# A ring of three banks, an argmax in six pieces partly on GpSimd, and another order in the attention's steps

## The chip, the cores and the metric

One core of one Trainium2 chip runs the kernel. The metric is the device time of one execution in microseconds, as the median of several runs. Below, PE is TensorE (PEld its weight loads), DVE is VectorE, ACT is ScalarE, POOL is GpSimd and SP is SyncE, whose queue issues nearly all DMAs.

## What is computed

A clustered attention, followed by two mixer layers that the change doesn't touch. The attention, for two batches of 8 heads, 768 positions and 64 numbers a head:

```
q_assign = np.argmax(np.einsum('bhsd,hcd->bhsc', q_n, c_n), axis=-1)
k_assign = np.argmax(np.einsum('bhsd,hcd->bhsc', k_n, c_n), axis=-1)
mask = q_assign[:, :, :, None] == k_assign[:, :, None, :]
scores = scale * np.matmul(q, k.transpose(0, 1, 3, 2))
scores = np.where(mask, scores, -1000000000.0)
scores = scores - np.max(scores, axis=-1, keepdims=True)
attn = np.exp(scores)
attn = attn / (np.sum(attn, axis=-1, keepdims=True) + 1e-09)
return np.matmul(attn, v).astype(np.float32)
```

Here `q_n`, `k_n` and `c_n` are the normed queries, keys and 16 centroids of a head. A position sees only the positions whose nearest centroid is the same as its own. The mixers are products of the result with `moe_*` and then `moe2_*` weights.

## The kernel before

Products of float32 numbers are made from a high part (rounded to fp32r) and a low part (what the rounding left over), so each tile is first split in two: ACT rounds, and DVE or POOL subtracts.

The attention runs over 8 pairs of heads (G = 8), and a pair is 12 steps of one tile of 128 query rows (NTT = 12, NTILE = 96 steps). The order of each engine's work is the order in which the program writes it; nothing is scheduled behind it. In `step(n)` the program writes: the score product of tile n+2 (`s_mm`) into one of two pairs of PSUM banks, its row maximum on DVE (`s_max`), the exponential of tile n+1 on ACT (`s_exp`) into one of three `p32` buffers, the six 128x128 transposes of tile n on PE (`t_mm`), four to a bank in two banks (TB), the split of each full bank (`t_out`: ACT writes `pth`, then DVE writes `ptl`), then the actions in `mid`, then two of the six chunks of the product with v of the three tiles before (`pv`, into bank OB, copied by `pv_out` after the third step), then the actions in `late`. Since six blocks fill one and a half banks, even and odd steps differ: an even step completes one bank, an odd step two.

`mid` and `late` are lists by step, filled by `at`: `merge` (12 small products that turn the result into rows, bank MB) and `merge_out` at two steps of each pair, `zmm` and `zadd` for the first mixer's low-rank part, and the preparation of a later pair. With s1 the first step of the pair ahead of pair n, that preparation is: load q and k (`load_pair`, s1-6), the products with the centroids (`scores`, s1-2), the high parts of q and k on ACT (s1-2 and s1-1), the transposition of the products to `am1` (`scores_out`) and the argmax on DVE (`argmax_a` at s1-1, `argmax_b` at s1), the low part of k on POOL (s1) and of q on DVE (s1+1), the mask rows (`mask_rows`, POOL, s1+1), and the DMAs that stack the parts into `qS` and `kS` (`stack`: eight for the high, six for the low parts, eight for the mask, on SP). The value tile is loaded at s1+3 and split at s1+5 (`v_split`: both halves on ACT, then on POOL).

The argmax takes the largest of each 16 products, marks the places that reach it, weighs the marks so that the first one wins, takes the largest again, marks it, and transposes the marks. Lines of the profile: 73 is every matrix product, 276 the transposes, 262 the row maximum, 267 the exponential, 78 every rounding on ACT, 85 every subtraction, 193 to 207 the argmax, 175 the load of v, 170 that of q.

## Time and profile before

| what | us |
|---|---|
| median of 3 runs (lowest, highest) | 872.11 (870.2, 873.57) |
| the profiled execution | 874.27 |
| its span, first to last instruction | 872.3 |
| PE busy in the span | 793.5 (91%) |
| DVE busy | 542.7 (62%) |
| ACT busy | 353.4 (41%) |
| POOL busy | 102.1 (12%) |

The mean granted clock of PE is 0.973 over the span. Shares over the span mix stages: the attention's steps run from 22 to 330 us, the mixers after that. Matmuls are pipelined, so a busy PE is not PE at its peak; how much of a stretch is lost is read from the waits ahead of its instructions and from the granted clock.

### The profile page before, as it was taken

Reading aid. Unit: us, or ns where it says so; the run is one execution under the profiler, and the core shown is the slowest. Engines: PE = TensorE matmul, PEld = TensorE weight load, DVE = VectorE, ACT = ScalarE, POOL = GpSimd, SP = SyncE. Lnnn points to the kernel's source line nnn. Section 1 sums busy time; section 2 is a strip of 40 time slices with the busy share of each in tenths; the row PEclk is TensorE's granted clock in tenths of the full one; section 3 lists DMA queues with packets and bytes.
Section 4 is the critical chain, followed back from the end, with each engine's and each line's share of the span. In section 5 each row is a group of like instructions: output and inputs, shape, how many; then the busy total and the mean of one; then the engine's idle time right before and its main releaser. Section 6 shows DMA issues by size and latency. Waiting matters only on the chain.

```text
span 872.3 us, 11264 instructions
## 1 busy us (share of the span) xinstructions
PE 793.5 (91%) x3989; PEld 666.1 (76%) x3989; DVE 542.7 (62%) x873; ACT 353.4 (41%) x687; POOL 102.1 (12%) x96
## 2 busy tenths in 40 slices
PE   1798888989889989988879999999999999999998
PEld 0677787878778877766558888788888888888886
DVE  3788868687787887888898687684233124113113
ACT  1686766667576664434333333342212121111110
POOL 1210101011110011000012232221210021000000
PEclk9998999999999989999989999999999999999999
DMA  8645334252535024888888999996444433754752
GB/s 209 138 109 136 73 100 92 81 116 79 151 80 153 25 97 146 279 284 285 286 291 309 367 354 393 390 388 231 145 153 166 140 125 132 276 194 159 274 193 96
DMA packets 59239, 167.79 MB, mean 192 GB/s; under 512 B 8656, under 2 KB 16848, under 8 KB 59184
## 3 DMA queue, kind: packets, MB, share of 16 engines
q1 hardware_dynamic: 57984, 164.95, 58.2%
q10 hardware_dynamic: 1200, 2.13, 1.0%
q8 instruction: 31, 0.51, 0.2%
q14 instruction: 24, 0.20, 0.1%
HBM read 114.10 MB, written 32.51 MB: 168 GB/s over the span
## 4 chain that ended last, share of the span: by engine, by line
PE 62%; DVE 23%; DMA 5%; ACT 4%; SPq 4%; issue 2%; DVEq 0%; ACTq 0%
PE ps L73 58%; PE ps L276 4%; DVE ptl L85 3%; DVE nm L262 3%; DVE c L104 3%; DVE c L105 3%; DVE qk L85 2%; ACT qk L78 2%; DVE c L100 2%; DVE c L103 2%; DMA qk<-scr_a 2%; DVE am L199 1%; DMA vraw<-in_v_dram 1%; SPq L239 1%; SPq L238 1%
## 5 line engine op out<-in xcount | busy, mean ns | idle before, releaser
L73 PE MATMUL ps<-gh,qk 128*128 128x512 f32 x672 | 223.7, 394 | 1.2 <-DMA qk<-scr_a 1.2
L610 DVE SCALAR_TENSOR_TENSOR gl<-ps,gh 128x512 fp32r<-128x512 f32 x84 | 57.9, 689 | 192.9 <-ACT gh L609 192.9
L73 PEld LDWEIGHTS ps<-gh,qk 128*128 128x128 f32 x672 | 127.2, 189 | 27.8 <-ACT gh L609 1.6
L609 ACT ACTIVATE gh<-ps 128x512 fp32r<-128x512 f32 x84 | 49.9, 594 | 225.8 <-PE ps L73 222.7
L73 PE MATMUL ps<-gl,qk 128*128 128x512 f32 x336 | 133.3, 397 | 4.0 <-DVE gl L610 3.4
L276 PE MATMUL ps<-ident,p 128*128 128x128 f32 x576 | 90.6, 290 | 27.0 <-DVE ptl L85 26.7
L73 PE MATMUL ps<-qk 112*128 112x384 f32 (+1 forms) x384 | 93.0, 368 | 23.4 <-ACT p L267 11.4
L262 DVE TENSOR_REDUCE nm<-ps 128x1 f32<-128x768 f32 x96 | 91.3, 951 | 28.4 <-PE ps L73 28.0
L85 DVE TENSOR_TENSOR ptl<-ps,pth 128x512 fp32r<-128x512 f32 x144 | 94.9, 685 | 21.5 <-ACT pth L78 18.3
L276 PEld LDWEIGHTS ps<-ident,p 128*128 128x128 f32 x576 | 73.1, 149 | 39.1 <-DVE ptl L85 35.4
L267 ACT ACTIVATE p<-ps,nm 128x768 f32<-128x768 f32 x96 | 86.5, 902 | 31.3 <-DVE nm L262 30.5
L78 ACT ACTIVATE pth<-ps 128x512 fp32r<-128x512 f32 x144 | 81.6, 597 | 43.1 <-PE ps L276 42.7
L73 PEld LDWEIGHTS ps<-qk 112*128 112x128 f32 (+1 forms) x384 | 74.8, 208 | 31.2 <-ACT p L267 18.2
L73 PE MATMUL ps<-qk,qk 128*128 128x512 f32 x336 | 86.2, 400 | 10.2 <-ACT qk L78 10.2
L73 PEld LDWEIGHTS ps<-qk,qk 128*128 128x128 f32 x336 | 61.0, 188 | 31.0 <-ACT qk L78 14.6
L73 PEld LDWEIGHTS ps<-gl,qk 128*128 128x128 f32 x336 | 63.6, 189 | 21.2 <-DVE gl L610 8.8
L73 PE MATMUL ps<-pth,vhl 128*128 128x384 f32 x192 | 76.7, 400 | 0.6 <-ACT osb L292 0.6
L73 PE MATMUL ps<-u2h,qk 128*128 128x512 f32 x224 | 74.1, 392 | 0.0
L73 PE MATMUL ps<-u1h,qk 128*128 128x512 f32 x224 | 73.9, 391 | 0.0
L78 ACT ACTIVATE qk<-c 128x512 fp32r<-128x512 f32 x56 | 35.3, 631 | 93.5 <-DVE c L105 60.6
L73 PE MATMUL ps<-ptl,vhl 128*128 128x384 f32 x192 | 68.5, 357 | 1.3 <-DVE ptl L85 1.3
L85 POOL TENSOR_TENSOR qk<-c,qk 128x512 fp32r<-128x512 f32 x28 | 39.5, 1410 | 150.9 <-ACT qk L78 150.9
(133 smaller groups left out, 1031.8 us busy)
## 6 DMA issues: line engine op xcount, KB each, us to landing
qk<-scr_b SPq DMA_DIRECT2D x72, 512.0 KB, 3.3
qk<-scr_a SPq DMA_DIRECT2D x64, 512.0 KB, 7.7
c<-in_wa_dram SPq DMA_DIRECT2D x32, 512.0 KB, 5.4
scr_a<-qk SPq DMA_DIRECT2D x32, 512.0 KB, 5.2
c<-in_wb_dram SPq DMA_DIRECT2D x24, 512.0 KB, 7.2
scr_b<-qk SPq DMA_DIRECT2D x24, 512.0 KB, 6.9
qk<-sq__84 SPq DMA_DIRECT2D x15, 384.0 KB, 3.9
qk<-sk__85 SPq DMA_DIRECT2D x29, 192.0 KB, 3.0
```

What stands on the lines that cost most here:

```text
L73: pe.matmul(o, lhsT=l, rhs=r, start=start, stop=stop, **kw)
L78: act.activation(o, i, AF.Copy, scale=scale)
L85: eng.tensor_tensor(out=o, in0=a, in1=b, op=ALU.subtract)
L100: dve.tensor_scalar(out=dst, in0=dst, scalar1=2.0 ** -15, scalar2=122879.9921875, op0=ALU.max, op1=ALU.min)
L103: dve.tensor_scalar(out=d, in0=d, scalar1=3, scalar2=0x3FFFFFF8, op0=ALU.logical_shift_left, op1=ALU.bitwise_and)
L104: dve.scalar_tensor_tensor(out=d, in0=lo, scalar=29, in1=d, op0=ALU.logical_shift_right, op1=ALU.bitwise_or)
L105: dve.scalar_tensor_tensor(out=d, in0=hi, scalar=-0x40000000, in1=d, op0=ALU.bitwise_and, op1=ALU.bitwise_or)
L262: dve.tensor_reduce(out=nm[:, n % 4 : n % 4 + 1], in_=ps[:, b0 : b0 + 2, 0:HS], axis=AX.XY, op=ALU.max, negate=True)
L267: act.activation(p32[n % NP32].rearrange("p (j k) -> p j k", j=2), ps[:, b0 : b0 + 2, 0:HS], AF.Exp, bias=nm[:, n % 4 : n % 4 + 1], accum_ ...
L276: pe.transpose(ps[:, TB + j % 2, ts(i, P)], p32[n % NP32][:, ts(c, P)], ident)
L609: act.activation(gh, o, AF.Relu)
L610: dve.scalar_tensor_tensor(out=gl, in0=o, scalar=0.0, in1=f32(gh), op0=ALU.max, op1=ALU.subtract)
```

## The change

`NP32` is 4. Transposes, `merge`, `scores`, `zmm` and `zadd` take their bank from a ring of banks 4, 5 and 6 in the order in which the program writes them; `pv` accumulates in bank 7. `t_out` is divided into `t_hi` (ACT) and `t_lo` (DVE). The argmax becomes `arg0` to `arg4`, which with `mask_rows` lie in different steps; in pairs 1 to 7 `arg1` and `arg3` run on POOL, where a comparison is a subtraction and a test of its sign. The preparation of a pair begins earlier (`load_pair` at s1-8, `scores` at s1-5), the load of v moves from s1+3 to s1-1, and the split of v is done in two halves, at s1+5 and s1+7. Pair 1's argmax is spread over steps 0 to 5, and its mask is stacked at step 6. `step` has one order for even steps and another for odd ones: in an even step `mid` runs right behind the score product and `late` ahead of `t_lo`; in an odd step two transposes come first, and the first `t_hi` comes ahead of the exponential.

```diff
-    NP32 = 3
+    NP32 = 4
...
-    def v_split(g):
+    def v_split(g, a):
         o, i = vhl[g % 2], vraw.rearrange("p c (a d) -> p a c d", a=2)
-        for a in range(2):
-            rnd(act, o[:, a, :, 0:D], i[:, a])
-            sub(pool, o[:, a, :, D:], i[:, a], f32(o[:, a, :, 0:D]))
+        rnd(act, o[:, a, :, 0:D], i[:, a])
+        sub(pool, o[:, a, :, D:], i[:, a], f32(o[:, a, :, 0:D]))
 
     held = {}
 
...
         p = g % NPAIR
-        held["sc"] = bk
+        held["sc"] = bk = ring()
         for qd in range(4):
             src = (Rq, Rk)[qd // 2]
             mm(ps[32 * qd : 32 * qd + 32, bk, 0:HS], zc[:, ts(p, 32)], src[:, ts(qd % 2, HS)], True, True)
...
 
-    def argmax_a():
-        v1 = am1.rearrange("p (g c) -> p g c", c=16)
-        v2 = am2.rearrange("p (g c) -> p g c", c=16)
+    v1 = am1.rearrange("p (g c) -> p g c", c=16)
+    v2 = am2.rearrange("p (g c) -> p g c", c=16)
+    v3_ = am3.rearrange("p (g c) -> p g c", c=16)
+    best = lambda: amx.unsqueeze(2).to_broadcast([P, 24, 16])
+
+    def arg0():
         dve.tensor_reduce(out=amx, in_=v1, axis=AX.X, op=ALU.max)
-        dve.tensor_tensor(out=v2, in0=v1, in1=amx.unsqueeze(2).to_broadcast([P, 24, 16]), op=ALU.is_ge)
-        dve.tensor_tensor(out=v2, in0=v2, in1=wcl.unsqueeze(1).to_broadcast([P, 24, 16]), op=ALU.mult)
-
-    def argmax_b():
-        v2 = am2.rearrange("p (g c) -> p g c", c=16)
-        v3_ = am3.rearrange("p (g c) -> p g c", c=16)
+
+    def arg1(eng):
+        w = wcl.unsqueeze(1).to_broadcast([P, 24, 16])
+        if eng is pool:
+            sub(pool, v1, v1, best())
+            pool.tensor_scalar(out=am2, in0=am1, scalar1=0.0, scalar2=None, op0=ALU.is_ge)
+            pool.tensor_tensor(out=v2, in0=v2, in1=w, op=ALU.mult)
+        else:
+            dve.tensor_tensor(out=v2, in0=v1, in1=best(), op=ALU.is_ge)
+            dve.tensor_tensor(out=v2, in0=v2, in1=w, op=ALU.mult)
+
+    def arg2():
         dve.tensor_reduce(out=amx, in_=v2, axis=AX.X, op=ALU.max)
-        dve.tensor_tensor(out=v3_, in0=v2, in1=amx.unsqueeze(2).to_broadcast([P, 24, 16]), op=ALU.is_equal)
+
+    def arg3(eng):
+        if eng is pool:
+            sub(pool, v2, v2, best())
+            pool.tensor_scalar(out=am3, in0=am2, scalar1=0.0, scalar2=None, op0=ALU.is_ge)
+        else:
+            dve.tensor_tensor(out=v3_, in0=v2, in1=best(), op=ALU.is_equal)
+
+    def arg4():
         dve.transpose(out=ohT, in_=am3)
 
     def mask_rows(eng):
...
 
-    TB, OB, MB = 4, 6, 7
+    OB = 7
+    banks, tb = [4, 5, 6], {}
+
+    def ring():
+
+        banks.append(banks.pop(0))
+        return banks[-1]
 
     def t_mm(n, c0, c1):
         for c in range(c0, c1):
             j, i = divmod(NS * n + c, 4)
-            pe.transpose(ps[:, TB + j % 2, ts(i, P)], p32[n % NP32][:, ts(c, P)], ident)
-
-    def t_out(j):
-        o = ps[:, TB + j % 2, :]
+            if i == 0:
+                tb[j] = ring()
+            pe.transpose(ps[:, tb[j], ts(i, P)], p32[n % NP32][:, ts(c, P)], ident)
+
+    def t_hi(j):
+        rnd(act, pth[:, ts(j % (NBL // 2), 4 * P)], ps[:, tb[j], :])
+
+    def t_lo(j):
         r = ts(j % (NBL // 2), 4 * P)
-        rnd(act, pth[:, r], o)
-        sub(dve, ptl[:, r], o, f32(pth[:, r]))
+        sub(dve, ptl[:, r], ps[:, tb[j], :], f32(pth[:, r]))
 
     def pv(k, c):
         g, h, a, _ = tinfo(NT * k)
...
 
-    def merge(g, h):
+    def merge(g, h, bk=None):
+        held["mg"] = bk = bk or ring()
         for t in range(NT):
             for a in range(2):
-                mm(ps[:, MB, t * P + a * D : t * P + a * D + D], osb[a][:, ts(t, P)], ii, True, True)
+                mm(ps[:, bk, t * P + a * D : t * P + a * D + D], osb[a][:, ts(t, P)], ii, True, True)
 
...
                     stack(0, a, what, (sp, act)[a], *l)
-            scores(0, MB)
+            scores(0)
             load_pair(1, act)
             scores_out()
-            argmax_a()
-            argmax_b()
+            arg0()
+            arg1(dve)
+            arg2()
+            arg3(dve)
+            arg4()
             mask_rows(dve)
             for a in range(2):
...
                 stack(1, a, "hi", sp)
-            v_split(0)
+            for a in range(2):
+                v_split(0, a)
             load_v(1)
             s_mm(0)
             s_mm(1)
             s_max(0)
             s_max(1)
-            scores(1, OB)
+            scores(1)
             scores_out()
             q_lo(dve, Rq)
...
             at(late, s, lambda g=g, h=h: merge_out(g, h))
         if g + 1 < G:
-            at(mid, s0 + NTT + 5, lambda g=g: zmm(g, MB))
+            at(mid, s0 + NTT + 5, lambda g=g: zmm(g, ring()))
             at(late, s0 + NTT + 5, lambda g=g: zmm_out(g))
         n, s1 = g + 1, s0
         if 2 <= n < G:
-            at(late, s1 - 6, lambda g=n: load_pair(g))
-            at(mid, s1 - 2, lambda g=n: scores(g, MB))
-            at(late, s1 - 2, q_hi)
-            at(late, s1 - 1, k_hi)
-            at(late, s1 - 1, scores_out)
-            at(late, s1 - 1, argmax_a)
-            at(late, s1, argmax_b)
-            at(late, s1, lambda: k_lo(pool, Rk))
-            for a in range(2):
-                at(late, s1, lambda g=n, a=a: stack(g, a, "hi", sp))
+            at(late, s1 - 8, lambda g=n: load_pair(g))
+            at(mid, s1 - 5, lambda g=n: scores(g))
+            at(late, s1 - 5, scores_out)
+            at(late, s1 - 4, q_hi)
+            at(late, s1 - 4, arg0)
+            at(late, s1 - 3, lambda: arg1(pool))
+            at(late, s1 - 2, k_hi)
+            at(late, s1 - 2, arg2)
+            at(late, s1 - 1, lambda: arg3(pool))
+            at(late, s1 - 1, lambda: k_lo(pool, Rk))
+            at(late, s1, arg4)
+            at(late, s1, lambda: q_lo(dve, Rq))
             at(late, s1 + 1, lambda: mask_rows(pool))
-            at(late, s1 + 1, lambda: q_lo(dve, Rq))
-            for a in range(2):
-                at(late, s1 + 2, lambda g=n, a=a: stack(g, a, "lo", sp))
-                at(late, s1 + 2, lambda g=n, a=a: stack(g, a, "mask", sp))
+            for what, s in (("hi", -2), ("lo", 1), ("mask", 2)):
+                for a in range(2):
+                    at(late, s1 + s, lambda g=n, a=a, w=what: stack(g, a, w, sp))
         if n < G:
             if n > 1:
-                at(late, s1 + 3, lambda g=n: load_v(g))
-            at(late, s1 + 5, lambda g=n: v_split(g))
+                at(late, s1 - 1, lambda g=n: load_v(g))
+            for a in range(2):
+                at(late, s1 + 5 + 2 * a, lambda g=n, a=a: v_split(g, a))
 
     for t in range(NS):
         s = NTT * 4 + 7 + 6 * t
-        at(mid, s, lambda t=t: zadd(0, t, MB))
-        at(late, s, lambda t=t: zadd_out(0, t, MB))
-    at(late, 0, argmax_a)
-    at(late, 1, argmax_b)
-    at(late, 1, lambda: mask_rows(dve))
+
+        def za(t=t):
+            held["za"] = ring()
+            zadd(0, t, held["za"])
+
+        at(mid, s, za)
+        at(late, s, lambda t=t: zadd_out(0, t, held["za"]))
+    for s, f in ((0, arg0), (1, lambda: arg1(pool)), (2, arg2), (3, lambda: arg3(pool)), (4, arg4), (5, lambda: mask_rows(pool))):
+        at(late, s, f)
     for a in range(2):
-        at(late, 1, lambda a=a: stack(1, a, "mask", sp))
+        at(late, 6, lambda a=a: stack(1, a, "mask", sp))
     at(late, 2, load_uv)
...
 
     def step(n):
-        if n + 2 < NTILE:
-            s_mm(n + 2)
-            s_max(n + 2)
-        if n + 1 < NTILE:
-            s_exp(n + 1)
+        k, r = divmod(n, NT)
         j, i = divmod(NS * n, 4)
-        t_mm(n, 0, 4 - i)
-        t_out(j)
-        t_mm(n, 4 - i, NS)
-        if i:
-            t_out(j + 1)
-        for f in mid.get(n, ()):
-            f()
-        k, r = divmod(n, NT)
-        if k:
-            for c in range(2 * r, 2 * r + 2):
-                pv(k - 1, c)
-            if r == 2:
+
+        def run(d):
+            for f in d.get(n, ()):
+                f()
+
+        def heads():
+            if n + 2 < NTILE:
+                s_mm(n + 2)
+
+        def maxima():
+            if n + 2 < NTILE:
+                s_max(n + 2)
+
+        def exps():
+            if n + 1 < NTILE:
+                s_exp(n + 1)
+
+        def pvs(*cs):
+            if k:
+                for c in cs:
+                    pv(k - 1, 2 * r + c)
+
+        def pvo():
+            if k and r == NT - 1:
                 pv_out(k - 1)
-        for f in late.get(n, ()):
-            f()
+
+        if i == 0:
+            heads()
+            run(mid)
+            t_mm(n, 0, 4)
+            pvs(0, 1)
+            maxima()
+            t_mm(n, 4, NS)
+            exps()
+            t_hi(j)
+            pvo()
+            run(late)
+            t_lo(j)
+        else:
+            t_mm(n, 0, 2)
+            heads()
+            maxima()
+            t_mm(n, 2, NS)
+            t_hi(j)
+            pvs(0)
+            t_lo(j)
+            pvs(1)
+            run(mid)
+            exps()
+            t_hi(j + 1)
+            t_lo(j + 1)
+            pvo()
+            run(late)
 
 
...
     hidden(0)
-    merge(G - 1, 1)
+    merge(G - 1, 1, 6)
     merge_out(G - 1, 1)
```

## Rows read from the trace of the kernel before

**Rows 1.** Stretches: length, busy time and instructions by engine, clock, DMA share, GB/s.

```profile
22.00:330.00 308.00, 268.85 (x1670) 242.73 (x1669) 249.61 (x377) 209.53 (x427) 36.96 (x32) 0.93 0.40 101
...
212.55:250.21 37.66, 33.45 (x216) 30.00 (x215) 30.79 (x48) 25.35 (x53) 4.46 (x4) 0.95 0.41 101
```

**Rows 2.** Timeline, TensorE's weight loads: start us, us, engine, line, what, count.

```profile
153.50 0.72 PEld L73 LDWEIGHTS ps<-qk 112*128 112x128 f32 x4
154.21 0.76 PEld L276 LDWEIGHTS ps<-ident,p 128*128 128x128 f32 x6
...
155.57 0.73 PEld L73 LDWEIGHTS ps<-qk 112*128 112x128 f32 x4
...
170.70 1.42 PEld L73 LDWEIGHTS ps<-ii,osb 128*128 128x128 f32 x12
```

**Rows 3.** PE's waits (us, times, longest): 22-330; 60-285 (two rows); 285-330.

```profile
PE ps L276 <- DVE ptl L85: 26.7, 17, 4.6
...
PE ps L276 <- DVE ptl L85: 17.6, 11, 4.6
PE ps L73 <- ACT p L267: 9.4, 6, 2.0
...
PE ps L276 <- DVE ptl L85: 5.2, 3, 2.4
```

**Rows 4.** Timeline of one argmax burst; in brackets: idle before, and what ended it.

```profile
179.47 1.83 POOL L85 TENSOR_TENSOR sk__85<-sk__85 128x768 fp32r<-128x768 f32 x1 [15.16 <-ACT sk__85 L78]
...
180.07 1.65 DVE L199 TENSOR_TENSOR am<-am,amx 128x384 bf16<-128x384 f32 x1
...
181.75 0.36 DVE L200 TENSOR_TENSOR am<-am,wcl 128x384 bf16<-128x384 bf16 x1
...
182.03 0.95 DVE L262 TENSOR_REDUCE nm<-ps 128x1 f32<-128x768 f32 x1
...
182.90 0.68 DVE L85 TENSOR_TENSOR ptl<-ps,pth 128x512 fp32r<-128x512 f32 x1
...
183.63 0.66 PE L276 MATMUL ps<-ident,p 128*128 128x128 f32 x4 [2.10 <-DVE ptl L85]
...
184.07 0.56 DVE L206 TENSOR_TENSOR am<-am,amx 128x384 bf16<-128x384 bf16 x1
```

**Rows 5.** Timeline around one load and split of v.

```profile
158.20 0.58 SPq L175 DMA_DIRECT2D vraw<-in_v_dram  x1
...
161.75 0.94 ACT L78 ACTIVATE vhl<-vraw 128x384 fp32r<-128x384 f32 x2 [1.23 <-DMA vraw<-in_v_dram]
...
163.62 1.51 PE L73 MATMUL ps<-qk 112*128 112x384 f32 x4 [1.96 <-ACT p L267]
```

**Rows 6.** Stretches at clock 0.50: two of ten, and all ten's sum.

```profile
163.81:167.22 3.41, 3.41 (x14) 3.32 (x14) 2.49 (x4) 2.50 (x6) 0.50 (x1) 0.50 0.00 0
...
320.82:327.65 6.83, 6.83 (x32) 6.73 (x31) 3.25 (x8) 2.90 (x7) 0.00 (x0) 0.50 0.09 34
sum 40.96, PE 39.30 PEld 37.53 DVE 32.06 ACT 24.04 POOL 3.83; mean PE 3.93 PEld 3.75 DVE 3.21 ACT 2.40 POOL 0.38
```

**Rows 7.** Groups by line, 212.55 to 250.21: count, busy us, mean ns, idle before.

```profile
L267 ACT ACTIVATE p<-ps,nm 128x768 f32<-128x768 f32 x12 | 10.8, 902 | 3.8 <-DVE nm L262 3.8
L78 ACT ACTIVATE pth<-ps 128x512 fp32r<-128x512 f32 x18 | 10.2, 596 | 5.2 <-PE ps L276 5.1
...
L85 POOL TENSOR_TENSOR vhl<-vraw,vhl 128x384 fp32r<-128x384 f32 x2 | 2.0, 1004 | 15.0 <-ACT vhl L78 15.0
...
L210 POOL TENSOR_SCALAR om<-ohT,msk 128x384 f32<-128x384 bf16 x1 | 0.7, 665 | 4.1 <-DVE ohT L207 4.1
```

**Rows 8.** Two lines on DVE: duration ns min/median/max, first and last start.

```profile
L199 DVE TENSOR_TENSOR am<-am,amx x8: 557/1646/1647, 10.9 to 254.9; 128x384 bf16<-128x384 f32 x8
...
L85 DVE TENSOR_TENSOR ptl<-ps,pth x142: 674/681/693, 30.0 to 326.1; 128x512 fp32r<-128x512 f32 x142
```

**Rows 9.** DMA issues, 22 to 330: KB each, median us to landing.

```profile
sq__84<-in_qT_dram SPq DMA_DIRECT2D x6, 384.0 KB, 3.9
```

## Prediction before the change was run

> **What bounds the kernel now.** The whole change lies in the attention stage, so I first read the busy time by stretch, then who waited for whom on TensorE inside that stage, then the clock granted there, and last one period of the timeline, to see which instruction stood late in which queue.
>
> The attention steps run from about 22 to 330 us, 308 of the 872. In that stretch TensorE is busy 269 us and the clock is 0.93 on average [rows 1]. In one pair's period of 37.66 us TensorE is busy 33.45, VectorE 30.79, ScalarE 25.35, GpSimd 4.46. No engine is full, but three are loaded, and each takes its work in program order. A step that nothing disturbs takes 155.57 - 153.50 = 2.07 us from one score product to the next, 0.71 of it the product and about 0.76 the six transposes [rows 2]; twelve of them are 24.8 us, and two merges of 1.42 raise it to 27.7. The rest of the period is small products and loss.
>
> Where the loss is: TensorE waited 26.7 us in 17 waits for `ptl`, the low half that VectorE takes out of a transpose bank [rows 3]. From 60 to 285 us these are 17.6 us in 11 waits, and beside them 9.4 us in 6 waits for ScalarE's exponential; from 285 to 330 us 5.2 us in 3. The two kinds have different causes.
>
> One: the argmax burst. `argmax_a` stands on VectorE as a block behind `scores_out` and ahead of the next row maximum. Its comparison takes 1.65 us while GpSimd runs `k_lo` (1.83), so the row maximum starts only at 182.03, the low half behind it at 182.90, and TensorE, whose only two transpose banks are both still to be read, sits idle 2.10 us until 183.63 [rows 4]. Six such waits stand between 60 and 285 us, the longest 4.6: 4.6 + 5 x 2.1 = 15.1 of the 17.6 us. The other five waits are short, 2.5 us together. Before 60 us 26.7 - 17.6 - 5.2 = 3.9 us of the same kind are left, from pair 1's argmax.
>
> Two: the v split. SyncE issues the load of v at 158.20, last behind the whole stack of the pair; ScalarE waits 1.23 us for it at 161.75, the exponential queues behind the split, and TensorE idles 1.96 us [rows 5]. Six times, 9.4 us.
>
> Three: the clock. Ten stretches, 40.96 us together, have a granted clock of 0.50 (1.2 GHz of 2.4); the one at 163.81 begins just after the wait that ended at 163.62 [rows 6]. Half of 40.96, some 20.5 us, is lost to that.
>
> **The change part by part.** *Ring of three banks.* Transposes get a third bank, the small products (merge, z, scores) share the ring, and `pv` keeps a bank of its own (7). With two banks a transpose needs the low half of two uses before; now of three. In even steps `late` stands ahead of `t_lo` on VectorE, which is a delay there, but only bank reuse three allocations later, or `pv` in the odd steps that begin a group, waits for that. I count the argmax waits as gone by this and the next part together and leave the five short ones (2.5 us) in.
>
> *Argmax.* VectorE loses three of its operations in each of pairs 2 to 7 and in pair 1: 1.65 + 0.36 + 0.56 = 2.57 us a pair [rows 4], 1.09 of it the time in which the comparison was held (it takes 0.557 at its shortest [rows 8]). Its load falls to 28.2 us a pair. GpSimd gets five: a subtraction of 384 columns (1.00 for the same size in `vhl`), a comparison (0.67 as `mask_rows`), a product (1.00), then a subtraction and a comparison: 2.67 and 1.67 us, 4.34 a pair [rows 7]. With its 4.46 it is busy some 9 of 33 us, so they lie beside other work. A comparison on GpSimd isn't in the trace: from below it is 0.67, from above 1.83, the longest GpSimd operation near it, though that has twice the columns [rows 4]; I take 0.67, the row of the same form. "GPSIMD Engine Reference", section 3.1, of the Trainium skill says that branching on data costs about 12 cycles an element; an estimate from it is 3.8 us for one comparison of 384 at its 1.2 GHz, which no run here shows, and with it the two GpSimd blocks would take 5.8 and 4.8 us instead of 2.7 and 1.7.
>
> The new waits: `arg2` and `arg4` on VectorE wait for GpSimd, and behind them in VectorE's queue stand the low half of an even step, and behind that the next row maximum, for which ScalarE and then TensorE wait. `arg2` is two steps behind `arg0`, one of them with a merge: 2 x 2.07 + 1.42 = 5.6 us for 2.67 us of work. `arg4` is two steps behind `arg2`: 4.1 us for 1.67. Both have more than 2 us to spare, so I cost them at nothing; without that cover each microsecond is a microsecond of the pair.
>
> *v split.* The load of v moves ahead of the low and mask stacks on SyncE's queue, past 14 issues of about 0.58 each [rows 5], so it lands some 8 us earlier against a wait of 1.23. The split becomes two pieces of half the length two steps apart. The six waits, 9.4 us, go. What is late next is the exponential behind one half of the split, in an odd step, where TensorE has transposes and a small product left.
>
> *SyncE's order.* `load_pair` goes from step -6 to -8 and `scores` from -2 to -5. Counted from `k_hi` at -2, the queue holds 7 + 1 + 6 + 8 issues and then the two loads, 24 x 0.58 = 13.9 us, plus 3.9 to land [rows 9]: 17.8 us. The scores come nine steps later, with one merge between: 9 x 2.07 + 1.42 = 20.0 us. It is covered by some 2 us and by the z product of that stretch; beyond that each late microsecond would stand on TensorE, with everything that is queued behind the scores. Pair 1's masks move from step 1 to 6; their eight issues take 8 x 0.58 = 4.6 us and are wanted at step 10, four steps or 8.3 us later. I cost it at nothing; without that cover it is a single wait.
>
> *Order in the step.* In an odd step ScalarE now has the high half of a two-block bank ahead of the exponential. Its chain is: two of the six transposes 0.25, high half 0.60, exponential 0.90 [rows 2, 7], 1.75 us, and then the next step's score product, which TensorE reaches at 2.07. That leaves 0.3 us for three hand-overs; the one from VectorE to TensorE in the burst takes 183.63 - 183.58 = 0.05 [rows 4], those from and to ScalarE aren't among these rows. So it is near the edge. From below it costs nothing; from above 0.4 us, as if a half of the high half stuck out. I take 0.1 in each of 48 odd steps, 4.8 us, near the lower end since 0.3 us stand against hand-overs of 0.05 each. A fourth `p32` buffer only frees the exponential.
>
> *The weight ticks and the last pair* are not touched: the 5.2 us there stay, and with them the stretch at half clock of 6.83 us [rows 6] and one more of 3.41 before it.
>
> **The sum.** Argmax waits 15.1 + 3.7 of pair 1 (of its 3.9, 0.2 is a short one), v waits 9.4: 28.2 us. Half clock: 40.96 - 6.83 - 3.41 = 30.7 us, of which half, 15.4, comes back when the waits ahead of these stretches are gone. Less 4.8: 38.8 us. Against the profiled execution's 874.3 that gives 835.5; this one is 2.2 above the median of 872.1, so for a median **833.3 us**. The rest of the kernel should shift as a whole: its weight conversion is tied to steps, not to a time.
>
> **The rivals.**
> *All of it.* The waits of both kinds and all half clock go: 26.7 + 9.4 + 20.5 = 56.6 us: 815.5. For it: the walk above finds no queue that is late. Against: the ticks and the last pair are as before.
> *ScalarE's order binds.* The chain of the odd step sticks out by 0.4: 48 x 0.4 = 19.2 in place of 4.8: 847.7. For: the 0.3 us of room. Against: steps with a merge or another small product at their end hide it.
> *GpSimd holds VectorE.* The comparison on VectorE took 1.65 while GpSimd worked and 0.557 alone [rows 4, 8]; such a hold is 1.09 us. If `q_lo` and the first operation of `merge_out` are held so in 7 pairs: 14 x 1.09 = 15.3, 848.6. Against: the low half, which reads PSUM, never took more than 0.693 in 142 [rows 8], and `k_lo` should be done before `q_lo` starts. "GPSIMD Engine Reference", section 8, of the Trainium skill says the same, that GpSimd shares its SBUF interfaces with VectorE and collides with operations that read two SBUF inputs; by that rule moving work to GpSimd costs VectorE part of what it saves.
> *VectorE waits for GpSimd: the slower end.* If the five new operations took much longer than their rows, `arg2` and `arg4` would stop VectorE with the low halves and row maxima behind them. It decides from 5.6 + 4.1 = 9.7 us for the five; the gain of 38.8 is eaten in 7 pairs at 9.7 + 5.5 = 15.2, some 3.0 us each. At 3.4 each, 17 us, it is 7 x 7.3 = 51 lost: 884. Against: no GpSimd operation of 384 columns in rows 7 is near that.
> *It doesn't do what it says.* The waits only change their name, another engine's queue being late each time: within 0.5% of 872, 868 to 876. Against: two of the three causes are removed at the source. A part of it, 852 to 868, is likelier.
>
> **How the numbers follow.** Forecast, 822 to 842: 0.50. All of it, 813 to 822: 0.10. ScalarE's order: 0.14. GpSimd holds VectorE: 0.12. A part only, 852 to 868: 0.06. No change: 0.03. Slower: 0.05. Faster by over 0.5% is then 0.92, within 0.5% (about what a measurement of this kernel can tell from no change) 0.03, slower 0.05. For 8 in 10 the range takes in most of the first rival and both at 848: 814 to 852.
>
> **What would show it.** Right: TensorE's waits for `ptl` from 60 to 285 us fall from 17.6 to under 4, those for the exponential from 9.4 to under 3 but for the odd steps, the half clock from 41 us to about 10, attention ends near 290 us, VectorE's busy time falls by some 18 us. Wrong: VectorE rows that wait for GpSimd (`arg2`, `arg4`), `q_lo` at 1.6 us, TensorE waiting for the load of q and k ahead of `scores`, or waits for the exponential in every other step. The prediction would be wrong if half-clock stretches come without long waits, or if the mixers start earlier and end at the same time.

## The result, and the profile after

The changed kernel takes 824.76 us (median of 4 runs, 823.29 to 826.56) where the kernel before, run beside it, takes 871.29 (4 runs): a ratio of 0.946, interval 0.944 to 0.949. Its profiled execution took 824.84 us. The forecast was 833.3, with a range of 814 to 852, so the gain came out 8.5 us larger than forecast.

First where the time went. The first hidden activation of the mixers starts at 291.58 us instead of 339.85, and the span is 49.5 us shorter (872.3 and 822.8): the attention stage gave all of it but a microsecond, and the rest shifted as a whole. The page's line of busy time of the kernel after:

```profile
PE 772.2 (94%) x3989; PEld 651.6 (79%) x3989; DVE 521.7 (63%) x851; ACT 349.1 (42%) x687; POOL 141.1 (17%) x132
```

Three stretches of it, two pairs and all attention steps (length; busy us and instructions of PE, PEld, DVE, ACT, POOL; clock; DMA share; GB/s):

```profile
179.80:210.87 31.07, 30.88 (x216) 28.38 (x215) 27.79 (x45) 24.99 (x53) 10.02 (x10) 1.00 0.51 122
89.02:119.20 30.18, 30.18 (x214) 28.02 (x213) 26.68 (x43) 24.64 (x53) 10.04 (x10) 1.00 0.51 126
22.00:281.00 259.00, 247.14 (x1673) 226.87 (x1671) 231.36 (x358) 206.88 (x430) 76.64 (x68) 0.98 0.49 123
```

The first is the pair (steps 60 to 72) that [rows 1] show: it takes 31.07 us instead of 37.66, and TensorE is busy in 30.88 of it at the full clock. VectorE's load of this pair fell from 30.79 to 27.79 (forecast 28.2), GpSimd's rose from 4.46 to 10.02. The second pair (steps 24 to 36) took 38.84 us in the kernel before and has no gap on TensorE now.

TensorE's waits on its matmul rows, 22 to 292 us (us in total, times, longest), of the kernel after:

```profile
PE ps L73 <- DVE ptl L85: 7.4, 5, 2.4
PE ps L73 <- ACT p L283: 4.2, 2, 2.4
...
PE ps L300 <- DVE ptl L85: 0.4, 2, 0.2
```

Of the 26.7 us for `ptl` and the 9.4 for the exponential in the middle pairs [rows 3] nearly all is gone; between 60 and 245 us only 0.4 for `ptl` and one wait of 2.4 for the exponential are left (245 us is about the step that stood at 285 in the kernel before). Of the 7.4, 6.5 stand in the weight ticks, the steps behind 245 us that also convert weights for the mixers. All matmul rows together fell by 26.1 us, from 40.2 (22 to 340 us) to 14.1. The same question put to the weight loads gives more. Up to the first hidden activation, the kernel before, 22 to 340 us:

```profile
PEld ps L276 <- DVE ptl L85: 35.4, 32, 4.8
PEld ps L73 <- ACT p L267: 18.2, 16, 3.0
PEld ps L73 <- issue: 7.8, 27, 0.6
PEld ps L73 <- DVE ptl L85: 1.6, 1, 1.6
PEld ps L73 <- ACT osb L292: 0.9, 1, 0.9
```

and the kernel after, 22 to 292 us:

```profile
PEld ps L73 <- DVE ptl L85: 10.4, 9, 2.6
PEld ps L73 <- ACT p L283: 5.8, 2, 3.0
PEld ps L73 <- DVE nm L278: 3.0, 12, 0.3
PEld ps L73 <- ACT vhl L78: 2.5, 4, 0.6
PEld ps L73 <- issue: 1.8, 8, 0.4
...
PEld ps L300 <- DVE ptl L85: 1.0, 2, 0.5
```

All rows of these two answers add up to 63.9 us before and 27.2 after, 36.7 less. At clock 0.50 there were 40.96 us up to the first hidden activation [rows 6]; now there are four stretches, two of them shown, with the sum of the four:

```profile
62.39:65.80 3.41, 3.41 (x14) 2.98 (x12) 3.37 (x5) 3.36 (x7) 0.36 (x1) 0.50 0.73 164
...
280.84:287.67 6.83, 5.51 (x16) 5.13 (x17) 3.33 (x8) 1.53 (x3) 0.44 (x1) 0.50 0.23 77
sum 17.07, PE 15.75 PEld 14.74 DVE 12.33 ACT 8.35 POOL 4.12; mean PE 3.94 PEld 3.69 DVE 3.08 ACT 2.09 POOL 1.03
```

Half of 40.96 - 17.07 is 12.0 us. 36.7 + 12.0 = 48.7, against the 48.3 us by which the mixers start earlier. (In the mixers the kernel before has one more stretch, 6.83 us from 450.53, and the kernel after one of 3.41 from 403.72.) This account, weight-load waits plus half of the half-clock time, is used for every run below.

The new argmax, timeline of GpSimd and VectorE in pair 3 of the kernel after (start us, us, engine, line, operation; in brackets the idle time before):

```profile
113.06 0.84 POOL L85 TENSOR_TENSOR am<-am,amx 128x384 f32<-128x384 f32 x1 [1.56 <-DVE amx L200]
113.99 1.17 POOL L206 TENSOR_SCALAR am<-am 128x384 bf16<-128x384 f32 x1
115.25 0.92 POOL L207 TENSOR_TENSOR am<-am,wcl 128x384 bf16<-128x384 bf16 x1
...
119.80 1.17 POOL L218 TENSOR_SCALAR am<-am 128x384 bf16<-128x384 bf16 x1
120.94 1.83 POOL L85 TENSOR_TENSOR sk__85<-sk__85 128x768 fp32r<-128x768 f32 x1
...
118.26 0.54 DVE L213 TENSOR_REDUCE amx<-am 128x24 f32<-128x384 bf16 x1
...
122.27 0.57 DVE L223 STREAM_TRANSPOSE ohT<-am 128x384 bf16<-128x384 bf16 x1
122.77 0.91 DVE L235 SCALAR_TENSOR_TENSOR sq__84<-sq__84 128x768 fp32r<-128x768 f32 x1
```

The first block on GpSimd ends at 116.17 and VectorE takes its result at 118.26, the second at 120.97 and 122.27: 2.1 and 1.3 us to spare. `k_lo` ends at 122.77, as `q_lo` (L235) starts, and that takes 0.91 us.

### The profile page after: what moved, and what is told of

It reads as the page before. It is cut to its first block, busy times and chain, and to the rows that moved or that the text cites. A ratio compares the mean times of both kernels' runs of the same rounds, so it can differ in the third digit from the quotient of the medians.

```text
span 822.8 us, 11265 instructions
## 1 busy us (share of the span) xinstructions
PE 772.2 (94%) x3989; PEld 651.6 (79%) x3989; DVE 521.7 (63%) x851; ACT 349.1 (42%) x687; POOL 141.1 (17%) x132
## 4 chain that ended last, share of the span: by engine, by line
PE 71%; DVE 19%; DMA 5%; ACT 3%; issue 1%; DVEq 0%; ACTq 0%; SPq 0%
PE ps L73 65%; PE ps L300 6%; DVE c L104 3%; DVE c L105 3%; DVE qk L85 2%; DMA qk<-scr_a 2%; ACT qk L78 2%; DVE ptl L85 2%; DVE c L103 2%; DVE nm L278 2%; DVE c L100 2%; PE ps L769 1%; DMA qk<-p 1%; ACT p L283 1%; DMA sk__85<-in_kT_dram 1%
## 5 line engine op out<-in xcount | busy, mean ns | idle before, releaser
L73 PEld LDWEIGHTS ps<-gh,qk 128*128 128x128 f32 x672 | 126.9, 189 | 27.3 <-ACT gh L679 1.2
L78 ACT ACTIVATE pth<-ps 128x512 fp32r<-128x512 f32 x144 | 86.2, 600 | 34.0 <-PE ps L300 33.4
L300 PE MATMUL ps<-ident,p 128*128 128x128 f32 x576 | 88.5, 276 | 0.5 <-DVE ptl L85 0.4
L73 PEld LDWEIGHTS ps<-qk 112*128 112x128 f32 (+1 forms) x384 | 66.4, 198 | 24.1 <-issue 13.6
L73 PE MATMUL ps<-pth,vhl 128*128 128x384 f32 x192 | 74.5, 388 | 1.0 <-ACT osb L317 1.0
```

Source lines behind the costliest of these rows:

```text
L73: pe.matmul(o, lhsT=l, rhs=r, start=start, stop=stop, **kw)
L78: act.activation(o, i, AF.Copy, scale=scale)
L300: pe.transpose(ps[:, tb[j], ts(i, P)], p32[n % NP32][:, ts(c, P)], ident)
```

## The experiments

Each run's account, with the figures worked out as above (us; "moved" is how much earlier than in the kernel before the first hidden activation starts):

| run | median | ratio, interval | moved | weight-load waits | at half clock | account |
|---|---|---|---|---|---|---|
| before | 871.3 | 1 | 0 | 63.9 | 41.0 | 0 |
| after | 824.8 | 0.946 (0.944 to 0.949) | 48.3 | 27.2 | 17.1 | 48.7 |
| b_v | 863.9 | 0.990 (0.987 to 0.992) | 9.5 | 62.8 | 27.3 | 8.0 |
| a_oldv | 833.3 | 0.954 (0.952 to 0.957) | 40.6 | 39.0 | 10.2 | 40.3 |
| a_block | 844.5 | 0.967 (0.964 to 0.969) | 27.0 | 43.2 | 30.7 | 25.9 |
| a_block_oldv | 844.9 | 0.967 (0.965 to 0.970) | 27.2 | 47.3 | 17.1 | 28.6 |
| a_dve | 832.5 | 0.954 (0.952 to 0.956) | 38.1 | 37.8 | 13.7 | 39.8 |
| a_2bank | 842.7 | 0.965 (0.962 to 0.968) | 29.2 | 45.4 | 20.5 | 28.8 |
| a_oldorder | 832.8 | 0.954 (0.952 to 0.956) | 39.7 | 34.8 | 13.7 | 42.8 |
| b_ring | 858.5 | 0.983 (0.979 to 0.988) | 12.3 | 54.6 | 34.1 | 12.8 |
| a_pool2 | 847.6 | 0.972 (0.969 to 0.974) | 24.3 | 45.3 | 27.3 | 25.5 |
| a_pool6 | 919.9 | 1.053 (1.050 to 1.057) | -46.5 | 96.5 | 92.2 | -58.2 |
| a_spread | 818.6 | 0.938 (0.936 to 0.940) | 53.6 | 26.0 | 6.8 | 55.0 |
| a_spread2 | 801.6 | 0.919 (0.915 to 0.922) | 57.1 | 23.5 | 0 | 60.9 |

Each ratio is taken against the kernel before as measured beside that run (medians 871.3 to 873.4 us), not against the first row. The account holds within 4 us but for a_pool6, so it doesn't price smaller differences; in a_pool6 long waits also lie inside the half-clock stretches, which would count them twice. My theory was that each cause in the prediction is real and costs about what the waits of [rows 3] say; the rivals were that the parts stand in for each other, or that one of them does it all.

**The v part alone, and the rest without it.** b_v is the kernel before with these lines; a_oldv is the kernel after with the opposite edit:

```diff
-                at(late, s1 + 3, lambda g=n: load_v(g))
-            at(late, s1 + 5, lambda g=n: v_split(g))
+                at(late, s1 - 1, lambda g=n: load_v(g))
+            for a in range(2):
+                at(late, s1 + 5 + 2 * a, lambda g=n, a=a: v_split(g, a))
```

> The kernel before with the v part of the change alone: the load of v moved from step +3 to -1 and its split in two halves at +5 and +7. Theory 1 (each of the two waits costs what TensorE's weight loads show of it): the weight loads waited 14.1 us in 12 waits for the exponential between 60 and 285 us, and two half-clock stretches begin behind these waits (3.4 us): 871 - 17 = 854, six waits for the exponential gone. Theory 2 (a queue that is late has a successor; the wait only changes its name, to VectorE's low halves): 866 to 871.

> The changed kernel with the v part undone: load of v at +3 behind the low and mask stacks, both halves of the split at +5. Theory 1: the wait of ScalarE for the load returns in pairs 2 to 7, 2 to 3 us each on TensorE: 837 to 845. Theory 2 (the new order and the third bank cover a late exponential): 825 to 829.

b_v gained 9.2 us (863.94 against 873.18), a_oldv lost 8.6 (833.34); both lie between the two expectations. In a_oldv the waits return where they were taken out, 75 to 245 us:

```profile
PE ps L300 <- ACT p L283: 6.6, 6, 1.7
```

In b_v the same six waits shrink to 0.35 us each, yet its weight-load waits fall only from 63.9 to 62.8; most of its gain is less time at half clock (27.3 for 41.0). In a_oldv it is the other way round: 11.8 us more of weight-load waits, and 6.9 less at half clock. So the part is worth 8 to 9 us, near the 9.4 of its waits, but a wait that is taken away comes back in part under another name while other causes remain. Nor does a given wait always cost the clock. The stretches of b_v around its argmax waits of 2.12 us (columns as above; the clock is the third from the end):

```profile
104.00:109.00 5.00, 2.97 (x19) 2.48 (x20) 4.86 (x9) 3.18 (x7) 0.66 (x1) 1.00 0.86 190
140.00:145.00 5.00, 4.39 (x19) 3.89 (x20) 4.86 (x8) 3.12 (x7) 0.66 (x1) 0.66 0.80 176
176.00:181.00 5.00, 3.66 (x23) 3.16 (x24) 4.86 (x9) 3.23 (x7) 0.66 (x1) 1.00 0.73 162
```

The wait itself, on TensorE's timeline, in the first two of them:

```profile
104.91 0.66 PE L275 MATMUL ps<-ident,p 128*128 128x128 f32 x4 [2.12 <-DVE ptl L85]
...
140.57 0.66 PE L275 MATMUL ps<-ident,p 128*128 128x128 f32 x4 [2.12 <-DVE ptl L85]
```

The same wait is followed by half clock at 140.57 and not at 104.91.

**The argmax as two blocks on VectorE,** with the new and with the old v part (a_block, a_block_oldv; pair 1 likewise):

```diff
-            at(late, s1 - 4, arg0)
-            at(late, s1 - 3, lambda: arg1(pool))
...
-            at(late, s1 - 2, arg2)
-            at(late, s1 - 1, lambda: arg3(pool))
+            at(late, s1 - 1, arg0)
+            at(late, s1 - 1, lambda: arg1(dve))
...
+            at(late, s1, arg2)
+            at(late, s1, lambda: arg3(dve))
```

> The changed kernel with the argmax as two blocks on VectorE at steps -1 and 0, as before; ring, order in the step and the v part stay. Theory 1 (the burst on VectorE is the cause, third bank and order soften it): 1 to 3 us a pair, 832 to 846. Theory 2 (the third bank alone removed the burst's cost): 825 to 827. Theory 3 (the pieces alone removed it): all of it back, 18.7 us and five half-clock stretches, 850 or more.

> Both undone: argmax as two blocks on VectorE, v part as before; what is left of the change is ring, order in the step and the earlier preparation. Theory 1 (the waits stand in different steps and add): the sum of the two runs above, 845 to 865. Theory 2 (they share their cover, so the first one hides the second): less than two thirds of that sum. Theory 3 (ring and order are the whole gain): 825 to 830.

In both, the halves of q and k keep their new steps. So these are not quite the blocks of the kernel before: `k_lo` is done ahead of the comparison, which takes 0.56 us and not 1.65, and `q_lo` (0.92) follows the second block at once.

a_block: 844.49, 19.7 us slower than after, in the range of its theory 1, though the third bank and the new order are there. Two terms make it, 16.0 more of weight-load waits and half of 13.6 more at half clock. a_block_oldv: 844.87, no slower than a_block, where the v part was worth 8.6 us beside the pieces; with 20.1 us it falls just outside theory 1 and above the two thirds of theory 2. Behind the block the v part is worth nothing: with it a_block has 4.1 us less of waits, but 13.6 us more at half clock. That is not one execution alone: the mean clock was 0.979 to 0.983 in a_block's four runs, 0.985 to 0.988 in the other's. Why the clock falls more often there stays open. The parts don't add.

**The pieces, all on VectorE** (a_dve), to tell the pieces from GpSimd:

```diff
-            at(late, s1 - 3, lambda: arg1(pool))
+            at(late, s1 - 3, lambda: arg1(dve))
...
-            at(late, s1 - 1, lambda: arg3(pool))
+            at(late, s1 - 1, lambda: arg3(dve))
```

> The changed kernel with the argmax in its pieces, but all of them on VectorE (arg1 and arg3 as in the kernel before). Theory 1 (what counts is that the burst is divided; VectorE is busy 26.7 of a pair's 30.2 us and has room for 1.5 to 2.6 more): 823 to 829. Theory 2 (the offload to GpSimd is needed): 1.5 to 2.6 us in 7 pairs, 835 to 843.

832.52, between the two. Of the 19.7 us that undoing both costs, 12.0 are the pieces and 7.8 that GpSimd does five of the operations.

**GpSimd slower** (a_pool2 runs each comparison three times over, a_pool6 seven times), to price the slower rival:

```diff
-            pool.tensor_scalar(out=am2, in0=am1, scalar1=0.0, scalar2=None, op0=ALU.is_ge)
+            for _ in range(3):
+                pool.tensor_scalar(out=am2, in0=am1, scalar1=0.0, scalar2=None, op0=ALU.is_ge)
```

> The changed kernel with each of the two comparisons on GpSimd written three times over (same result), 2 x 1.17 us more in each block. In the changed kernel's trace the block ends 2.1 us before arg2 starts and 1.3 us before arg4. Theory 1 (VectorE's waits for GpSimd are covered that far, and TensorE has a little cover behind that): arg2 0.2 late, arg4 1.0 and the low part of q held behind the low part of k, 1 to 2 us in 7 pairs on VectorE, half of it on TensorE: 825 to 834. Theory 2 (GpSimd's work costs VectorE as it runs, by shared interfaces): 4.7 us in 7 pairs, 850 or more.

> The same with each comparison seven times over, 7.0 us more in each block. Theory 1: arg2 comes 4.9 us late and arg4 5.7, 10.6 us in 7 pairs less 1 to 2 of cover each: 885 to 899, slower than before the change, and VectorE's rows show the waits for GpSimd. Theory 2 (VectorE's lateness is absorbed by the third bank and the pieces' distance): 850 or less.

a_pool2 took 847.58, 22.8 more, which neither theory gave; a_pool6 took 919.86, slower than the kernel before and 21 us beyond theory 1. VectorE's timeline in one pair of a_pool2:

```profile
126.74 0.55 DVE L214 TENSOR_REDUCE amx<-am 128x24 f32<-128x384 bf16 x1 [0.35 <-POOL am L208]
...
132.00 0.58 DVE L225 STREAM_TRANSPOSE ohT<-am 128x384 bf16<-128x384 bf16 x1 [1.19 <-POOL am L220]
132.50 2.08 DVE L237 SCALAR_TENSOR_TENSOR sq__84<-sq__84 128x768 fp32r<-128x768 f32 x1
```

VectorE's waits in a_pool6, 75 to 330 us:

```profile
DVE ohT L225 <- POOL am L220: 34.9, 6, 6.2
DVE amx L214 <- POOL am L208: 26.9, 5, 5.4
```

In a_pool2 VectorE waits only 1.5 us a pair; beside that `k_lo` on GpSimd now runs next to `q_lo`, which takes 2.08 us instead of 0.91, and a half-clock stretch follows in five pairs. The rival's mechanism exists, and it is dear: from a_pool2 to a_pool6 each microsecond a pair cost (95.1 - 22.8) / (14.0 - 4.7) = 7.8 us over the 7 pairs, with 4.7 and 14.0 the added GpSimd time of a pair (4 and 12 comparisons of 1.17). On a straight line between the two runs, an estimate, the gain of 46.5 is gone at about 7.8 us more a pair, 12.7 us for the five operations that take 4.94; my prediction had 15.2.

**Transposes on two banks again,** the small products on the third (a_2bank; the `zadd` products move one step later):

```diff
-    banks, tb = [4, 5, 6], {}
+    banks, tb = [4, 5], {}
...
     def ring():
+        return 6
...
-                tb[j] = ring()
+                tb[j] = ring2()
```

> The changed kernel with transposes on two banks (4 and 5) and all small products on bank 6; for that, the zadd steps are one later. Theory 1 (the third bank matters only where VectorE is in arrears, which is seldom now): 825 to 833. Theory 2 (in the new order t_lo stands behind the late work in even steps, so with two banks the first transposes of the odd step after wait each time): 0.3 us or more in 48 steps, 840 or more.

842.66, 17.9 more than after: the rival's size, but not evenly spread. TensorE's waits, 75 to 245 us and 245 to 305:

```profile
PE ps L302 <- DVE ptl L85: 3.7, 5, 0.8
...
PE ps L302 <- DVE ptl L85: 12.4, 4, 5.2
```

In the middle pairs, where the pieces leave VectorE no burst, transposes wait 3.7 us where the kernel after has 0.4; in the weight ticks at the end, where VectorE still has bursts, they wait 12.4, where after has 6.5 for `ptl` on other products. The weight-load rows, by which the account goes, divide it otherwise. In the middle pairs, 75 to 245 us:

```profile
PEld ps L302 <- DVE ptl L85: 9.7, 16, 1.1
```

All weight-load rows of that stretch are 16.7 us against 7.8 in the kernel after, half of the 18.2 that two banks add in all. So the third bank is a buffer against the bursts and, in 16 short waits over some 60 steps, against a late low half between them; theory 2 had a wait in every odd step.

**The order of the step, and the ring alone.** a_oldorder puts the old order into the kernel after; b_ring gives the kernel before the ring, the fourth `p32`, the earlier loads and scores and the new steps for the halves of q and k, with blocks as in a_block, old v and old order:

```diff
+        heads()
+        maxima()
+        exps()
+        t_mm(n, 0, 4 - i)
+        t_hi(j)
+        t_lo(j)
...
+        run(mid)
+        pvs(0, 1)
+        pvo()
+        run(late)
```

> The changed kernel with the old order in the step (score product, row maximum, exponential, transposes and splits, mid, pv, late, the same in even and odd steps); ring, pieces and v part stay. Theory 1 (order matters little once the bursts are divided): 825 to 835. Theory 2 (the order is what lets TensorE run without a gap): transposes wait for the exponential written just ahead of them, 0.2 to 0.4 us a step, 843 to 863.

> Of the change only the ring of three banks with the fourth p32 buffer and the earlier load and scores; argmax in two blocks on VectorE, v part and order in the step as before. Theory 1 (with blocks on VectorE the order is worth little, since VectorE sets the pace there): 843 to 853, near the run with both undone. Theory 2 (ring and order only work together): 860 to 872. Theory 3 (the ring alone is nearly all of what these two gave): 840 to 848.

a_oldorder: 832.82, in the range of theory 1, so the new order gains 8.1 us. b_ring: 858.47, a gain of 14.9 against 873.39 beside it, and in none of the three ranges: 5.5 us slower than theory 1 allows and 1.5 faster than theory 2. What a_block_oldv has beyond it is the order alone, 858.5 - 844.9 = 13.6. The order is worth some 13.6 beside blocks and 8.1 beside pieces; b_ring's four runs lie 7.0 us apart, so the first figure is rough.

**What is left spread out too.** In the kernel after, the wait that ends at 62.02 us begins with the conversion of V, most of which stands on VectorE in one step:

```profile
55.78 1.84 POOL L85 TENSOR_TENSOR sk__85<-sk__85 128x768 fp32r<-128x768 f32 x1
...
56.44 1.60 DVE L103 TENSOR_SCALAR xn<-xn 96x768 int32<-96x768 int32 x1
...
58.07 0.95 DVE L104 SCALAR_TENSOR_TENSOR xn<-xn 96x768 int32<-96x768 int32 x1
...
59.94 0.95 DVE L278 TENSOR_REDUCE nm<-ps 128x1 f32<-128x768 f32 x1
...
60.98 0.90 ACT L283 ACTIVATE p<-ps,nm 128x768 f32<-128x768 f32 x1 [2.63 <-DVE nm L278]
```

L103 takes 1.60 us beside `k_lo` on GpSimd (the first line); in the kernel before it takes 0.55.

a_spread divides the conversions into single operations a step and each weight tick into three parts. a_spread2 divides the split of V's rows as well, puts the rounding and low half of a weight block (`stage(n - 4, 4)`) behind the first bit operations of a tick, where they stood ahead of them, and moves the low half of the first four blocks from GpSimd to VectorE:

```diff
-        return [magnitude, clamp, bits]
+        return [magnitude, clamp, bits, bits2, bits3]
...
-        at(late, NTILE - 20 + 3 * i, tick)
+        for x in range(3):
+            at(late, NTILE - 22 + 3 * i + x, subtick)
...
-                sub(pool if k < 4 or k >= 2 * NFA else dve, o[:, 1, :], r32, f32(o[:, 0, :]))
+                sub(pool if k >= 2 * NFA else dve, o[:, 1, :], r32, f32(o[:, 0, :]))
...
+            for part_ in range(3):
...
+                if part_ == 1 and 0 <= n - 4 < len(blocks):
+                    stage(n - 4, 4)
```

> The changed kernel with the remaining bursts divided too: the conversion of U and V one VectorE operation a step (V from step 13 on, its split at 19), and each weight tick of the last two pairs in three parts, one a step. Theory 1 (what is left of waits in pair 1 and in the last pair is the same kind of burst): the wait of 2.4 at 62 us, those of 1.6, 1.8 and 0.7 at 252 to 272 and two half-clock stretches, 3.4, go: 816 to 820. Theory 2 (these waits are the load of VectorE as a whole, not its bursts): 824 to 826.

> The spread kernel once more divided: the split of V one operation a step, and in the weight ticks the low part of the first blocks on VectorE beside its other parts instead of on GpSimd, which held a VectorE clamp for 1.1 us. Theory 1 (the waits of 2.0 us at 250 and 272 and the 1.0 at 79 come from these holds and this burst): 813 to 817. Theory 2 (VectorE is simply full in the last pair): 817 to 821, as the run it starts from.

a_spread: 818.55, as expected in time, but mostly by the clock: time at half clock falls from 17.1 to 6.8 us, weight-load waits only from 27.2 to 26.0. The wait of 2.4 at 62 is gone; those of 1.6 and 1.8 at 251.8 and 271.8 stand as 2.0 and 2.1. a_spread2: 801.64, 11 us under its expectation and the fastest of all, 23.1 us below the changed kernel. Its attention has no half clock left. Only 8.8 us of the 23.1 by which its span is shorter than after's lie ahead of the first hidden activation. From the first to the 31st hidden activation 13.4 more are gained (192.8 and 179.4). TensorE's waits in the mixers of the kernel after, 300 to 400 us:

```profile
PE ps L73 <- ACT qk L78: 9.8, 11, 1.1
```

and the same row of a_spread2, 290 to 392 us:

```profile
PE ps L73 <- ACT qk L78: 0.6, 2, 0.4
```

Nine of eleven regular waits for ScalarE's rounding of the weights vanish, 9.2 of the 13.4 us; the wait of 3.45 us for VectorE that ends at 403.46 and the half-clock stretch behind it are 1.43 us (at 381.07) and none in a_spread2. I had not aimed at these. The division of the tick is not the cause, since a_spread has it and keeps them, 295 to 395 us:

```profile
PE ps L73 <- ACT qk L78: 9.7, 11, 1.1
```

Nor is it the engine of the low half: in the kernel after, GpSimd sits idle from 288.5 to 397.84, so that the low halves of these blocks are VectorE's in both kernels:

```profile
397.84 1.55 POOL L85 TENSOR_TENSOR t1l<-c,t1h 128x512 fp32r<-128x512 f32 x1 [109.33 <-ACT t1h L78]
```

What is left is the order within the tick; it was not undone by itself.

## Why the prediction was right, and where its sum was off

The forecast was 833.3 and the result 824.8; "all of it" at 815.5 lies about as far on the other side. In the terms of the sum, 38.8 us were forecast and the account has 48.7: waits 36.7 for 28.2, half clock 12.0 for 15.4, and nothing lost by the order where 4.8 were taken off. That the misses of 8.5 and 4.8 one way and 3.4 the other cancel in part is luck. Step by step:

*Argmax waits gone: right, but one of them was not all argmax.* From 60 to 245 us the waits for `ptl` on matmul rows are 0.4 us (forecast under 4 where 17.6 stood). a_block and a_2bank show that it took both, as the prediction assumed when it counted them together: with either missing, 16 to 18 us more of weight-load waits stand. The longest of the six waits, 4.6 us, was read as an argmax burst. VectorE's and TensorE's timeline in the kernel before:

```profile
62.98 1.65 DVE L199 TENSOR_TENSOR am<-am,amx 128x384 bf16<-128x384 f32 x1
...
64.93 0.55 DVE L103 TENSOR_SCALAR xn<-xn 96x768 int32<-96x768 int32 x1
65.52 0.95 DVE L104 SCALAR_TENSOR_TENSOR xn<-xn 96x768 int32<-96x768 int32 x1
66.50 0.95 DVE L105 SCALAR_TENSOR_TENSOR xn<-xn 96x768 int32<-96x768 int32 x1
...
68.98 1.12 PE L276 MATMUL ps<-ident,p 128*128 128x128 f32 x4 [4.55 <-DVE ptl L85]
```

Behind the argmax stands the conversion of V, 0.55 + 0.95 + 0.95 = 2.45 us, just what this wait has beyond the 2.10 of the others. The change left that conversion in one step, and the kernel after has a wait of 2.43 us at 62.02 behind it, now put down to the exponential.

*v waits gone: right*, with the term of 9.4 against 8.6 and 9.2 measured. The waits went and come back as said, but that the times agree with the term is partly luck: in b_v most of the gain is clock, and in a_oldv the clock gives back a part of the 11.8 us of waits. In a_block, behind the blocks, the part was worth nothing.

*The size of the waits: too small.* The term of 28.2 us was read on TensorE's matmul rows. On those rows 26.1 us went, near the term. On the weight-load rows 36.7 went, and this with the clock accounts for the shift. The profile's page says that the ends of matmuls are modelled, so a matmul row may cover part of a wait; that this is the reason is argued, the two sums are measured. The Trainium skill, "Perfetto Trace Analysis", section "Identifying the Most-Contended Engine", calls matmul busy time a poor measure of how close a kernel is to its limit and sends the reader to the busy share of weight loads. It speaks of busy time and not of waits; for waits this trace points the same way, with 36.7 us against 26.1.

*Order on ScalarE, -4.8: wrong in sign.* In the kernel after, from 75 to 245 us, no matmul and no weight load waits for the exponential, so the chain of 1.75 in 2.07 us has room. Undoing the order cost 8.1 us. In a_oldorder the weight loads of that stretch wait 6.3 us for `ptl` and 4.0 for the exponential, against 2.2 and none. The prediction weighed only what the order delays on ScalarE, not which waits it takes away.

*Half clock, 15.4 back: 12.0.* Forecast was about 10 us of stretches left, and 17.1 are. The weight ticks keep theirs, as said; the two others make up the 3.4 us that are missing. The one at 62.39 follows the wait behind the conversion, which the prediction took for argmax. The one at 28.25 follows a wait of 1.76 us for an exponential that ends at 26.80; the kernel before has that wait too (1.69 us) without such a stretch.

*GpSimd: the price was too low, the cover held.* A comparison took 1.17 us, not 0.67; the subtraction and the product took 0.84 and 0.92, not 1.00. The five are 4.94 us a pair against 4.34. The Trainium skill, "GPSIMD Engine Reference", section 3.1, has branching on data at some 12 cycles an element, by which I had estimated 3.8 us; with 1.17 measured, that price doesn't hold for this comparison. 2.1 and 1.3 us of the cover were left, so no VectorE row of the attention's steps waits for GpSimd. At 3.8 us the two waits would have been real: a_pool2, at 3.5 us for each comparison three times, lost half of the gain.

*GpSimd holds VectorE: not where the rival put it.* `q_lo` takes 0.91 us, and 1.69 once, in pair 1, where it starts beside the low half of v on GpSimd (1.63 in the kernel before); in the later pairs `k_lo` ends as it starts (120.94 + 1.83 = 122.77 us), so with nothing to spare. The hold came elsewhere: the conversion L103 at 56.44 takes 1.60 us beside `k_lo` where it took 0.55, which is 1.05 of the burst ahead of the wait of 2.43. a_pool2 shows what the rival needs in every pair: `k_lo` beside `q_lo` makes that 2.08.

*SyncE's order at nothing: right.* In one pair the load of q goes out at 104.76, and in none does a TensorE row wait for a load of q or k. VectorE's busy time fell 21.0 us (forecast some 18), and attention ends near 281, where about 290 was forecast. What was not foreseen is that the parts don't add: undone one by one they cost 8.6, 19.7, 17.9 and 8.1 us, 54.3 in all, more than the 46.5 of the whole change: some parts, as the pieces and the third bank, take away the same waits only together.

## What to carry to other kernels

When several engines take their work in program order, look for operations issued as a block behind a late event, and issue them one a step: here that was worth 12 us for the argmax with the same engine doing the work, and another 6 for the conversions of U, V and the weights, most of that by the clock. Read TensorE's waits on its weight-load rows as well, and price a changed order by what it takes out of the way, not only by what it delays. Parts of such a change depend on each other: two may work only together (pieces and third bank), or one may be worth less beside another (the order beside the pieces). So undo them one at a time, and don't take what one costs when undone for its share of the gain.

## What the runs showed of the hardware that was not expected

GpSimd can be held by VectorE, and not only the other way round: the masks on GpSimd (L226) take 0.66 us at their shortest and 1.27 beside `q_lo`, which itself is not held. Durations (min, median, max ns) of the two in the kernel after:

```profile
L226 POOL TENSOR_SCALAR om<-ohT,msk x7: 656/1268/1270, 41.3 to 214.6; 128x384 f32<-128x384 bf16 x7
...
L235 DVE SCALAR_TENSOR_TENSOR sq__84<-sq__84 x7: 912/914/1694, 25.6 to 214.4; 128x768 fp32r<-128x768 f32 x7
```

The Trainium skill, "GPSIMD Engine Reference", section 8, says that the two share SBUF interfaces; the trace agrees, with both taking turns at being the one held (0.66 to 1.27 here, 0.91 to 2.08 in a_pool2). In both it is the later one: here `q_lo` starts at 122.77 and the mask at 122.95, in a_pool2 `k_lo` at 131.93 and `q_lo` at 132.50. And in b_v a wait of the same 2.12 us is followed by half clock in two of five pairs and not in the others, so single waits are no measure of what the clock costs.
